# Attention probabilities times values in plain float32, and bias work moved between the engines, in an attention + two-MoE kernel

## The chip, the cores and the metric

The kernel runs on one core of a Trainium2 chip. The metric is device time in microseconds of one execution. A profile gives one execution's span, first to last recorded instruction, and its own time, which is a little longer. The engines are named as in the profile: PE (TensorE matmul), PEld (TensorE weight load), DVE (VectorE), ACT (ScalarE), POOL (GpSimd), SP (the queue that issues most DMAs).

## The reference

Attention with a learned relative-position bias, then two mixture-of-experts layers. The change touches the attention alone:

```python
scores = scale * np.matmul(q, k.transpose(0, 1, 3, 2))
x = (psi_rel / psi_i)[..., None]
bias = np.maximum(x @ w1 + b1, 0.0) @ w2
scores = scores + bias.transpose(2, 0, 1)[None, :, :, :]
attn = np.exp(scores - np.max(scores, axis=-1, keepdims=True))
attn = attn / (np.sum(attn, axis=-1, keepdims=True) + 1e-09)
out = np.matmul(attn, v).astype(np.float32)
```

There are 2 batches, 8 heads, 576 positions and a head width of 64. The result, 1152 rows of 512, goes through `_moe_ref` and `_moe2_ref` (8 experts each, 512 to 1024 to 512).

## The kernel before

**Tiles.** The query rows are cut into 9 tiles of 128: tiles 0 to 7 are one block of 128 positions of one batch each, tile 8 holds the last 64 positions of both batches. Two tiles in a row share one bias block (`it = t // 2`). The loop in `attention` walks over 72 heads (tile, head), and for each one these steps are written out, the scores three heads ahead and the product with V two heads behind:

- `s_mm`: scores, 4 PE matmuls of 288 columns (8 in tile 8), fp32r, Q in two parts against K (L321)
- `s_max`: DVE adds the bias and takes the row maximum (L329)
- `s_exp`: ACT takes the exponential and the row sum (L339)
- `p_turn`: 4 PE transposes of the probabilities, 128x128 float32, into PSUM (L353)
- `p_hi`, `p_lo`: ACT writes the transposed probabilities, times 4096, as float16 (`pth`, L359); DVE writes what float16 left out (`ptl`, L364)
- `av`: for each of 4 chunks of 128 keys, three float16 matmuls of 64 columns: `pth` with VH, `pth` with VL, `ptl` with VH (L382)

The last 64 keys of two neighbouring heads form a "remainder" of 128 rows; it is transposed, split and multiplied once a tile (`av` with h = H, 128 columns). Then `finish` scales by 1/sum (L396), and `x_tile` transposes the tile and makes the router's logits (L683, L692: the latter is a product of two plain float32 operands, 4 matmuls a tile).

**Bias.** The bias of one block is made in 18 pieces of 32 keys (9 in the last block). For each piece DVE makes a mask (L246, L249), PE multiplies it with 16 matmuls into one PSUM tile (L259), and `bias_out` combines it: by default ACT copies it to SBUF (L271) and POOL does a product and a sum (L272, L273); a `direct` piece is read from PSUM by two DVE instructions (L267, L268). Block 0 is made ahead of the loop ("the start"), with pieces 5, 9 and 13 direct; the later blocks are made inside the loop, none direct. The PSUM tile `pm` of the loop has one buffer.

**V and Q.** In the start V is loaded raw (`vraw`, `vrem`), its largest magnitude is found (`v_sums` on ACT, `v_scale`), and `v_split`, `v_rem` write a scaled float16 part on ACT (L302, L310) and the rest on DVE (L303, L311). `q_split` makes Q's fp32r part on ACT (L152) and the low part on POOL (L153). `k_split` does the same for K on ACT and DVE (L166, L167), two pieces in the start and six in the first 11 heads.

**Order.** A scheduler puts the instructions of the loop in a fixed order on each engine; each engine runs its list in order and waits where an operand is not ready. The end of the loop (last heads of tile 8) is in an order written out by hand.

Of the kernel before, what the change touches and what calls it, by code (L numbers as in the profile page):

```python
# [20 lines left out]
BH = B * H
# [6 lines left out]
PSC = 4096.0  # L28
EXPM = 0x7F800000
KCH = 2  # L30
VC = BH * 4 * D // 4
VAT = 11, 13, 15, 17
DIRECT = 5, 9, 13
# [62 lines left out]
def attention(tc, ctx, g, a, out, setup, on_tile, on_slot):  # L96
# [14 lines left out]
    VH = keep.tile([P, BH, 4, D], F16, name="VH")  # L111
    VL = keep.tile([P, BH, 4, D], F16, name="VL")
    VRH = keep.tile([P, BH // 2, 2, D], F16, name="VRH")
    VRL = keep.tile([P, BH // 2, 2, D], F16, name="VRL")
# [35 lines left out]
    def q_split(t):  # L150
        for b, qr, Q in tiles[t].qs:
            nc.scalar.copy(Q[:, 0], qr)  # L152
            nc.gpsimd.tensor_tensor(Q[:, 1], qr, Q[:, 0].bitcast(F32), ALU.subtract)  # L153
# [32 lines left out]
    vraw = prep.tile([P, BH * 4 * D], F32, name="vraw")  # L186
    for x in range(2):
        nc.sync.dma_start(vraw[:, x * 2 * VC:(x + 1) * 2 * VC], a["a_v"][:, x * 2 * VC:(x + 1) * 2 * VC])
    vrem = prep.tile([P, BH // 2, D], F32, name="vrem")
    nc.sync.dma_start(vrem, a["a_vr"].rearrange("p (t d) -> p t d", d=D))  # L190
# [89 lines left out]
    def v_sums(vm, x):  # L280

        junk = prep.tile([P, VC], F16, tag="junk", name="junk", bufs=2)
        src = vraw[:, x * VC:(x + 1) * VC] if x < 4 else vrem.rearrange("p a d -> p (a d)")
        nc.scalar.activation(junk[:, :src.shape[1]], src, AF.Abs, accum_out=vm[:, x:x + 1])

    def v_scale(vm, stage_):
        if stage_ == 0:
            nc.vector.tensor_reduce(vm[:, 5:6], vm[:, 0:5], AX.X, ALU.max)
            v_scale.p = psA.tile([P, 512], F32, tag="acc", name="pv")
            nc.tensor.transpose(v_scale.p[0:1, 0:P], vm[:, 5:6], ident)  # L290
            v_scale.v1 = prep.tile([1, 1], F32, name="v1")
            nc.vector.tensor_reduce(v_scale.v1, v_scale.p[0:1, 0:P], AX.X, ALU.max)
            return
        nc.tensor.matmul(v_scale.p[:, P:P + 1], g.ones[0:1, :], v_scale.v1, start=True, stop=True)
        vmx = prep.tile([P, 1], F32, name="vmx")
        nc.vector.tensor_copy(vmx, v_scale.p[:, P:P + 1])
        return pow2_scales(nc, keep, vmx, "sv")

    def v_split(x):
        cs = slice(x * VC, (x + 1) * VC)  # L300
        vh = VH.rearrange("p a b d -> p (a b d)")[:, cs]
        nc.scalar.mul(vh, vraw[:, cs], sv)  # L302
        nc.vector.scalar_tensor_tensor(VL.rearrange("p a b d -> p (a b d)")[:, cs], vraw[:, cs], sv, vh, ALU.mult, ALU.subtract)  # L303

    def v_rem():
        nc.gpsimd.memset(VRH, 0.0)
        nc.gpsimd.memset(VRL, 0.0)
        for r in range(2):
            rr = slice(r * 64, r * 64 + 64)
            nc.scalar.mul(VRH[rr, :, r], vrem[rr], sv[rr])  # L310
            nc.vector.scalar_tensor_tensor(VRL[rr, :, r], vrem[rr], sv[rr], VRH[rr, :, r], ALU.mult, ALU.subtract)  # L311


# [41 lines left out]
    def p_hi(t, h, ccs=slice(0, 4)):  # L355
        o = tiles[t]
        if h not in o.av:
            o.av[h] = [late.tile([P, 4, P], F16, tag=f"pt{x}", name="pt" + x, bufs=5) for x in "hl"]
        nc.scalar.mul(o.av[h][0][:, ccs], o.pt[h][:, ccs], PSC)  # L359

    def p_lo(t, h, ccs=slice(0, 4)):
        o = tiles[t]
        th, tl = o.av[h]
        nc.vector.scalar_tensor_tensor(tl[:, ccs], o.pt.pop(h)[:, ccs], PSC, th[:, ccs], ALU.mult, ALU.subtract)  # L364

    def av(t, h, ccs=range(4)):
        o = tiles[t]
        if h == 0:
            o.acc = psA.tile([P, 512], F32, tag="acc", name="acc")
        th, tl = o.av[h]  # L370
        for cc in ccs:
            for b, _, _ in o.qs:
                ii = slice(0, P) if t < 8 else slice(b * 64, b * 64 + 64)
                pos = None if t < 8 else (0, b * 64)
                if h < H:
                    cs = slice(h * D, (h + 1) * D)
                    vh, vl = VH[:, b * H + h, cc], VL[:, b * H + h, cc]
                else:
# [73 lines left out]
    for si, u in enumerate(heads[:-4]):  # L452
# [13 lines left out]
        p_lo(*u)  # L466
# [49 lines left out]
    with tc.manual_schedule():  # L516
# [4 lines left out]
        p_hi(t, 4)  # L521
        p_lo(t, 4)
# [3 lines left out]
        p_hi(t, 5)  # L526
        p_lo(t, 5)
# [3 lines left out]
        p_hi(t, 6)  # L531
        p_lo(t, 6)
# [740 lines left out]
```

## Time and profile before

| | |
|---|---|
| median of 3 runs | 659.82 us (657.37 to 660.79) |
| profiled execution, its own time | 658.62 us |
| its span | 656.7 us |
| PE, DVE, ACT, POOL busy in the span | 551.3, 475.0, 400.8, 343.3 us |

The busy time of PE overstates it: matmuls overlap, and one that issues every 0.03 us is shown with a duration of 0.19 us. How long PE is taken by a piece of work is read from the distance between starts. The attention takes the first 256 us of the span.

### The profile page before, as it was taken

What the parts mean: (1) busy time and instruction counts of PE and PEld (TensorE: products, weight loads), DVE (VectorE), ACT (ScalarE), POOL (GpSimd) and SP (SyncE); (2) the same over time, 40 slices, a digit from 0 to 9 for tenths busy, and PEclk for the clock granted to TensorE, in tenths of its full rate; (3) what the DMA queues carried; (4) which work ended last, traced back from release to release, by engine and by line L of the source; (5) the groups of instructions that cost most, each with busy time, mean ns of one, the idle gap of its engine ahead of it and who ended that gap; (6) DMA issues with size and microseconds to landing.
All of it is one profiled execution on the core that took longest, in us unless ns stands there. A gap on an engine that the chain in (4) does not pass through costs nothing. (4 is left out here: it accounts for less than half of the span.)

```text
span 656.7 us, 13255 instructions
## 1 busy us (share of the span) xinstructions
PE 551.3 (84%) x4970; PEld 463.6 (71%) x4970; DVE 475.0 (72%) x702; ACT 400.8 (61%) x668; POOL 343.3 (52%) x290
## 2 busy tenths in 40 slices
PE   2446688887898999679999999989979999999892
PEld 2445577887887887467788788767757887777672
DVE  5789999999998886868951371289679725929660
ACT  4566877887888855358742443378527626648451
POOL 3997899988987262634552141144145513525430
PEclk9977988999999999889999999999999999999797
DMA  7922545101100772298971270168737734847700
GB/s 228 308 74 51 142 133 165 38 30 37 25 18 18 164 267 80 81 324 302 326 284 44 59 252 30 35 211 316 276 102 241 277 126 147 302 150 233 267 8 8
DMA packets 46871, 101.46 MB, mean 154 GB/s; under 512 B 10740, under 2 KB 12660, under 8 KB 46496
## 3 DMA queue, kind: packets, MB, share of 16 engines
q1 hardware_dynamic: 40640, 92.12, 43.2%
q0 software_dynamic: 5232, 7.49, 3.3%
q8 instruction: 64, 1.05, 0.7%
q14 instruction: 55, 0.45, 0.2%
q10 hardware_dynamic: 880, 0.35, 0.2%
HBM read 94.06 MB, written 13.67 MB: 164 GB/s over the span
## 5 line engine op out<-in xcount | busy, mean ns | idle before, releaser
L906 DVE TENSOR_TENSOR wl<-raw,wh 128x1024 fp32r<-128x1024 f32 x106 | 155.1, 1499 | 22.4 <-ACT wh L893 17.4
L959 PE MATMUL py<-wh,hT 128*128 128x512 f32 x400 | 141.4, 404 | 0.3 <-DVE hT L989 0.2
L893 ACT CAST wh<-raw 128x1024 fp32r<-128x1024 f32 x111 | 114.8, 1050 | 12.5 <-ACTq L1161 4.4
L989 DVE TENSOR_TENSOR hT<-pt,hT 128x512 fp32r<-128x512 f32 x50 | 34.5, 691 | 92.7 <-ACT hT L988 92.6
L272 POOL TENSOR_TENSOR btmp<-abst,xp 128x256 f32<-128x256 f32 x78 | 81.0, 1038 | 16.4 <-ACT abst L271 15.2
L959 PEld LDWEIGHTS py<-wh,hT 128*128 128x128 f32 x400 | 75.0, 188 | 16.0 <-DVE hT L989 1.1
L259 PE MATMUL pm<-wmov,mask 128*128 128x64 f16 x1296 | 58.7, 204 | 28.4 <-DVE wmov L234 12.3
L959 PE MATMUL py<-wl,hT 128*128 128x512 f32 x200 | 78.2, 391 | 0.0
L259 PEld LDWEIGHTS <-mask 128*128 128x128 f16 x1296 | 52.9, 106 | 33.5 <-DVE mask L246 22.9
L321 PE MATMUL s<-K,Q 128*128 128x288 f32 x320 | 64.2, 326 | 13.8 <-DVE mx L329 10.3
L273 POOL TENSOR_TENSOR bias<-abst,btmp 128x256 f32<-128x256 f32 x78 | 72.0, 923 | 5.8
L246 DVE TENSOR_TENSOR mask<-toep,T 128x1024 f16<-128x1024 f16 x72 | 69.6, 984 | 0.8 <-PE pm L259 0.5
L339 ACT ACTIVATE P<-sb,mx 128x576 f32<-128x576 f32 x72 | 55.8, 776 | 23.0 <-DVE mx L329 19.3
L271 ACT ACTIVATE abst<-pm,swi 128x512 f32<-128x512 f32 x78 | 53.0, 685 | 21.9 <-PE pm L259 20.6
L959 PE MATMUL ph<-wh,xh 128*128 128x512 f32 x120 | 52.1, 434 | 15.6 <-PEq L1161 10.2
L353 PE MATMUL pt<-ident,P 128*128 128x128 f32 x324 | 53.5, 287 | 9.5 <-DVE ptl L364 6.0
L329 DVE CUSTOM_DVE_ANT_0 sb<-s,bias 128x576 f32<-128x576 f32 x72 | 53.7, 748 | 8.0 <-PE s L321 4.5
L364 DVE SCALAR_TENSOR_TENSOR ptl<-pt,pth 128x512 f16<-128x512 f32 x81 | 54.8, 680 | 5.2 <-ACT pth L359 5.0
L321 PEld LDWEIGHTS s<-K,Q 128*128 128x128 f32 x320 | 47.7, 198 | 15.1 <-issue 9.2
L906 POOL TENSOR_TENSOR wl<-raw,wh 128x1024 fp32r<-128x1024 f32 x22 | 52.7, 2398 | 6.2 <-ACT wh L893 5.5
L359 ACT ACTIVATE pth<-pt 128x512 f16<-128x512 f32 x81 | 47.6, 592 | 8.4 <-PE pt L353 7.1
L988 ACT CAST hT<-pt 128x512 fp32r<-128x512 f32 x50 | 29.4, 587 | 34.3 <-PE pt L983 30.4
(216 smaller groups left out, 1191.0 us busy)
## 6 DMA issues: line engine op xcount, KB each, us to landing
raw<-m_w_dram SPq DMA_DIRECT2D x64, 512.0 KB
raw<-n_w_dram SPq DMA_DIRECT2D x64, 512.0 KB
kraw<-a_k_dram SPq DMA_DIRECT2D x16, 288.0 KB
qraw<-a_q_dram SPq DMA_DIRECT2D x16, 256.0 KB
out_dram<-zero SPq DMA_DIRECT2D x9, 256.0 KB
y_tok<-zero SPq DMA_DIRECT2D x9, 256.0 KB
vraw<-a_v_dram SPq DMA_DIRECT2D x2, 1024.0 KB
x_tok<-x SPq DMA_DIRECT2D x8, 256.0 KB
```

Of the source, the lines that this page charges most:

```text
L246: nc.vector.tensor_tensor(m, w, T[:, i0:i0 + P].unsqueeze(1).to_broadcast([P, 8, P]), ALU.is_gt)
L259: nc.tensor.matmul(pm[:, :, :, gq * 4:gq * 4 + 4], m[:, gq], wmov[:, part], start=part == 0, stop=part == 1)
L272: nc.gpsimd.tensor_tensor(tmp, ab_[:, 0], xp, ALU.mult)
L273: nc.gpsimd.tensor_tensor(biases[it][:, :, cs], ab_[:, 1], tmp, ALU.add)
L321: nc.tensor.matmul(ps[:, half, :288], Q[:, part, h], K[:, b * H + h, half * 288:half * 288 + 288], start=i == 0, stop=i == last)
L329: nc.vector.tensor_tensor_reduce(sb.rearrange("p (t j) -> p t j", t=2), o.ps.pop(h)[:, :, :288], biases[o.it][:, h].rearrange("p (t j) -> ...
L339: nc.scalar.activation(o.Pt[hp][:, x * S:(x + 1) * S], sb, AF.Exp, bias=mx, scale=-1.0, accum_out=o.sums[:, h:h + 1])
L353: nc.tensor.transpose(pt[:, cc], src, ident)
L364: nc.vector.scalar_tensor_tensor(tl[:, ccs], o.pt.pop(h)[:, ccs], PSC, th[:, ccs], ALU.mult, ALU.subtract)
L893: eng.copy(hi, r)
L906: eng.tensor_tensor(lo, self.raw.pop((ge, j)), hi.bitcast(F32), ALU.subtract)
L959: self.nc.tensor.matmul(ps, x[a_][:, xs], w[b_][:, ws], start=first and i == 0, stop=last and i == 2)
```

## The change

The split of V into two float16 parts and the search for its scale are gone: V is loaded as float32 into the tile that the matmuls read (`V_`, and `VR` for the remainder, which is zeroed on POOL and loaded by two DMAs of 64 partitions instead of one of 128). The probabilities are copied from PSUM as float32 by one instruction (`p_out`) on ACT, in the hand-written end for three of the five on DVE; there is no low part. `av` then has one plain float32 matmul for each chunk where there were three in float16. Every second bias piece is `direct` (8 of 18 in the start, every odd one in the loop), and Q's low part is made by DVE for all tiles but the first.

```diff
-DIRECT = 5, 9, 13
+DIRECT = 1, 3, 5, 7, 9, 11, 13, 15
-    VH = keep.tile([P, BH, 4, D], F16, name="VH")
-    VL = keep.tile([P, BH, 4, D], F16, name="VL")
-    VRH = keep.tile([P, BH // 2, 2, D], F16, name="VRH")
-    VRL = keep.tile([P, BH // 2, 2, D], F16, name="VRL")
+    V_ = keep.tile([P, BH, 4, D], F32, name="V")
+    VR = keep.tile([P, BH // 2, 2, D], F32, name="VR")
...
-            nc.gpsimd.tensor_tensor(Q[:, 1], qr, Q[:, 0].bitcast(F32), ALU.subtract)
+            (nc.vector if t else nc.gpsimd).tensor_tensor(Q[:, 1], qr, Q[:, 0].bitcast(F32), ALU.subtract)
...
+    for b in range(B):
+        nc.sync.dma_start(V_[:, b * H:(b + 1) * H].rearrange("p a c d -> p (a c d)"), a["a_v"][:, b * H * 4 * D:(b + 1) * H * 4 * D])
+    nc.gpsimd.memset(VR, 0.0)
+    for r in range(2):
+        rr = slice(r * 64, r * 64 + 64)
+        nc.sync.dma_start(VR[rr, :, r], a["a_vr"][rr].rearrange("p (t d) -> p t d", d=D))
...
+    def p_out(t, h, eng=nc.scalar):
+        o = tiles[t]
+        o.av[h] = late.tile([P, 4, P], F32, tag="pT", name="pT", bufs=5)
+        (eng.copy if eng is nc.scalar else eng.tensor_copy)(o.av[h], o.pt.pop(h))
...
-                for i, (l_, r_) in enumerate(((th, vh), (th, vl), (tl, vh))):
-                    nc.tensor.matmul(o.acc[ii, cs], l_[:, cc, ii], r_, start=h == 0 and cc == 0 and i == 0, stop=i == 2,
-                                     tile_position=pos, skip_group_check=True)
+                nc.tensor.matmul(o.acc[ii, cs], pT[:, cc, ii], v, start=h == 0 and cc == 0, stop=True,
+                                 tile_position=pos, skip_group_check=True)
...
-        nc.vector.tensor_scalar(r, o.sums, 1e-9, PSC, ALU.add, ALU.mult)
+        nc.vector.tensor_scalar(r, o.sums, 1e-9, None, ALU.add)
         nc.vector.reciprocal(r, r)
-        nc.vector.tensor_scalar(r, r, isv, None, ALU.mult)
...
-        if 4 <= x < 9:
-            v_sums(vm, x - 4)
-        if x == 9:
-            v_scale(vm, 0)
-        if x == 10:
-            sv, isv = v_scale(vm, 1)
-        if x in VAT:
-            v_split(VAT.index(x))
-        if x == 16:
-            v_rem()
...
-            bias_out(*w)
+            bias_out(*w, w[1] % 2 == 1)
...
-        p_hi(*u)
+        p_out(*u)
...
-        p_lo(*u)
```

The scheduler gives another order of instructions. Line numbers of the kernel after the change differ from those before. At three places:

On DVE at the end of the start, before the change, up to the first row maximum (`sb,mx`); VL and VRL are the low parts of V:

```order
L267 SCALAR_TENSOR_TENSOR btmp<-pm,swi,xp 128x256
L246 TENSOR_TENSOR mask<-toep,T 128x1024
L268 SCALAR_TENSOR_TENSOR bias<-pm,swi,btmp 128x8x32
L303 SCALAR_TENSOR_TENSOR VL<-vraw,svs,VH 128x1024 x3
L311 SCALAR_TENSOR_TENSOR VRL<-vrem,svs,VRH 64x8x64 x2
L303 SCALAR_TENSOR_TENSOR VL<-vraw,svs,VH 128x1024
L661 COPY enT<-pt 128x32
L329 ISA sb,mx<-s,bias 128x576
```

And the same place after it (L263 and L264 are the direct pieces, L242 the masks, L162 K's low part, L291 the row maximum):

```order
L263 SCALAR_TENSOR_TENSOR btmp<-pm,swi,xp 128x256
L162 TENSOR_TENSOR K<-kraw,K 64x1152
L264 SCALAR_TENSOR_TENSOR bias<-pm,swi,btmp 128x8x32
L242 TENSOR_TENSOR mask<-toep,T 128x1024 x2
L263 SCALAR_TENSOR_TENSOR btmp<-pm,swi,xp 128x256
L242 TENSOR_TENSOR mask<-toep,T 128x1024
L264 SCALAR_TENSOR_TENSOR bias<-pm,swi,btmp 128x8x32
L597 COPY enT<-pt 128x32
L242 TENSOR_TENSOR mask<-toep,T 128x1024
L291 ISA sb,mx<-s,bias 128x576
```

The six instructions on V are gone, and between the masks stand pairs that read a bias piece from PSUM; two of the last masks shown belong to block 1 already. On POOL in the start, `ess` (a small power that DVE needs for `en`) stood behind Q's low part, before the change:

```order
L306 MEMSET VRH 128x1024
L307 MEMSET VRL 128x1024
L153 TENSOR_TENSOR Q<-qraw,Q 128x1024
L653 TENSOR_TENSOR ess<-ess,half 8x1
L272 TENSOR_TENSOR btmp<-abst,xp 128x256
```

and stands ahead of it after the change:

```order
L183 MEMSET VR 128x1024
L589 TENSOR_TENSOR ess<-ess,half 8x1
L148 TENSOR_TENSOR Q<-qraw,Q 128x1024
L268 TENSOR_TENSOR btmp<-abst,xp 128x256
L269 TENSOR_TENSOR bias<-abst,btmp 128x8x32
```

So the small power no longer waits for the long subtraction. On DVE in the loop, at a reciprocal of the row sums in the middle of the attention, before the change (L364 is `p_lo`):

```order
L364 SCALAR_TENSOR_TENSOR ptl<-pt,pth 128x512
L246 TENSOR_TENSOR mask<-toep,T 128x1024
L388 TENSOR_SCALAR rinv<-sums 128x8
L329 ISA sb,mx<-s,bias 128x576
L329 ISA mx 128x1
L364 SCALAR_TENSOR_TENSOR ptl<-pt,pth 128x512
L246 TENSOR_TENSOR mask<-toep,T 128x1024
L389 RECIPROCAL rinv<-rinv 128x8
```

and at such a place after it:

```order
L242 TENSOR_TENSOR mask<-toep,T 128x1024
L148 TENSOR_TENSOR Q<-qraw,Q 128x1024
L263 SCALAR_TENSOR_TENSOR btmp<-pm,swi,xp 128x256
L242 TENSOR_TENSOR mask<-toep,T 128x1024
L264 SCALAR_TENSOR_TENSOR bias<-pm,swi,btmp 128x8x32
L343 TENSOR_SCALAR rinv<-sums 128x8
L344 RECIPROCAL rinv<-rinv 128x8
```

The `ptl` instructions are gone; Q's low part and the direct bias pairs have come, each pair with a mask between its two instructions.

## Rows read from the trace of the kernel before

**Rows 1.** The page: the span.

```profile
span 656.7 us, 13255 instructions
```

**Rows 2.** By stretch: us, busy PE, PEld, DVE, ACT, POOL (x count), PEclk, DMA, GB/s.

```profile
12.00:53.00 41.00, 19.68 (x319) 17.76 (x319) 32.98 (x51) 24.62 (x37) 38.27 (x33) 0.86 0.60 191
53.00:118.80 65.80, 51.06 (x776) 46.03 (x776) 63.81 (x102) 51.30 (x96) 58.09 (x51) 0.91 0.46 122
118.80:205.70 86.90, 74.24 (x1305) 68.72 (x1306) 84.78 (x159) 73.09 (x151) 74.52 (x78) 1.00 0.10 28
205.70:240.30 34.60, 32.79 (x458) 30.49 (x455) 29.03 (x69) 27.00 (x61) 19.24 (x16) 1.00 0.65 189
```

**Rows 3.** Timeline of PE: starts of successive blocks in the loop.

```profile
113.76 0.66 PE L353 MATMUL pt<-ident,P 128*128 128x128 f32 x4 [0.83 <-DVE ptl L364]
114.17 0.78 PE L321 MATMUL s<-K,Q 128*128 128x288 f32 x4
114.79 0.20 PE L382 MATMUL acc<-VH,pth 128*128 128x64 f16 x1
...
115.15 0.22 PE L382 MATMUL acc<-VRH,pth 128*128 128x128 f16 x1
...
115.82 0.63 PE L259 MATMUL pm<-wmov,mask 128*128 128x64 f16 x16
116.29 0.64 PE L353 MATMUL pt<-ident,P 128*128 128x128 f32 x4
```

**Rows 4.** Timeline of PE's weight loads: L692's plain float32 operands, and float16.

```profile
101.67 0.97 PEld L692 LDWEIGHTS s<-enT,xT 128*128 128x128 f32 x8 [1.56 <-DVE mx L329]
...
151.35 0.63 PEld L259 LDWEIGHTS <-mask 128*128 128x128 f16 x16
```

**Rows 5.** All of L692, in the whole span.

```profile
L692 PEld LDWEIGHTS s<-enT,xT x72: 186/192/192, 101.7 to 256.3; 128*128 128x128 f32 x72
```

**Rows 6.** Waits between 118.8 and 205.7 us, in total, times, longest.

```profile
PE acc L382 <- DVE ptl L364: 5.3, 4, 1.5
...
PE pm L259 <- ACT abst L271: 3.3, 4, 1.8
```

**Rows 7.** Timeline of DVE in the start.

```profile
17.05 0.14 DVE L654 TENSOR_SCALAR ess<-ess 8x1 f32<-8x1 f32 x1 [2.79 <-POOL ess L653]
...
18.77 1.89 DVE L246 TENSOR_TENSOR mask<-toep,T 128x1024 f16<-128x1024 f16 x3
20.69 1.77 DVE L167 TENSOR_TENSOR K<-kraw,K 64x1152 fp32r<-64x1152 f32 x1
...
42.40 0.47 DVE L267 SCALAR_TENSOR_TENSOR btmp<-pm,swi,xp 128x256 f32<-128x256 f32 x1
42.79 0.69 DVE L246 TENSOR_TENSOR mask<-toep,T 128x1024 f16<-128x1024 f16 x1
...
53.02 0.76 DVE L329 CUSTOM_DVE_ANT_0 sb<-s,bias 128x576 f32<-128x576 f32 x1 [0.51 <-POOL bias L273]
```

**Rows 8.** POOL's two bias instructions between 12 and 53 us.

```profile
L272 POOL TENSOR_TENSOR btmp<-abst,xp 128x256 f32<-128x256 f32 x15 | 18.0, 1202 | 0.5
L273 POOL TENSOR_TENSOR bias<-abst,btmp 128x256 f32<-128x256 f32 x15 | 16.6, 1108 | 1.2
```

**Rows 9.** DVE between 118.8 and 205.7 us, by line; and a subtraction of Q's shape.

```profile
L246 DVE TENSOR_TENSOR mask<-toep,T 128x1024 f16<-128x1024 f16 x28 | 27.9, 1005 | 0.1
...
L364 DVE SCALAR_TENSOR_TENSOR ptl<-pt,pth 128x512 f16<-128x512 f32 x36 | 24.4, 678 | 0.1
...
L390 DVE TENSOR_SCALAR rinv<-rinv,svi 128x8 f32<-128x8 f32 x4 | 2.6, 655 | 0.0
...
280.22 1.22 DVE L906 TENSOR_TENSOR wl<-raw,wh 128x1024 fp32r<-128x1024 f32 x1
```

**Rows 10.** Timeline of PE in tile 8: first and last row of one head's product.

```profile
241.49 0.23 PE L382 MATMUL acc<-VH,pth 128*64 128x64 f16 x2
...
241.99 0.66 PE L683 MATMUL pt<-ident,x 128*128 128x128 f32 x4
```

More of the change, by code (lines that the diff above doesn't have):

```diff
@@ L27 @@
 NPC = S // 32
-PSC = 4096.0
 EXPM = 0x7F800000
 KCH = 2
-VC = BH * 4 * D // 4
-VAT = 11, 13, 15, 17
-DIRECT = 5, 9, 13
+DIRECT = 1, 3, 5, 7, 9, 11, 13, 15
 XSTEP = 1, 2, 3, 4
@@ L185, in attention @@
     k_load(0)
[L186 to L190, printed above, removed]
+    for b in range(B):
[4 more added lines that the diff above has]
+        nc.sync.dma_start(VR[rr, :, r], a["a_vr"][rr].rearrange("p (t d) -> p t d", d=D))
     k_load(1)
@@ L277, in bias_out @@
             nc.sync.dma_start(biases[4][64:128, :, 0:288], biases[4][0:64, :, 0:288])
[L280 to L311, printed above, removed]
     def s_mm(t, h):
@@ L353, in p_turn, with av @@
             nc.tensor.transpose(pt[:, cc], src, ident)
-    def p_hi(t, h, ccs=slice(0, 4)):
+    def p_out(t, h, eng=nc.scalar):
         o = tiles[t]
[L357 to L366, printed above, removed]
+        o.av[h] = late.tile([P, 4, P], F32, tag="pT", name="pT", bufs=5)
+        (eng.copy if eng is nc.scalar else eng.tensor_copy)(o.av[h], o.pt.pop(h))
+    def av(t, h):
         o = tiles[t]
@@ L369, in av @@
             o.acc = psA.tile([P, 512], F32, tag="acc", name="acc")
-        th, tl = o.av[h]
-        for cc in ccs:
+        pT = o.av.pop(h)
+        for cc in range(4):
             for b, _, _ in o.qs:
@@ L376, in av @@
                     cs = slice(h * D, (h + 1) * D)
-                    vh, vl = VH[:, b * H + h, cc], VL[:, b * H + h, cc]
+                    v = V_[:, b * H + h, cc]
                 else:
                     cs = slice(cc * P, (cc + 1) * P)
-                    vh, vl = (V_[:, b * 4 + cc].rearrange("p t d -> p (t d)") for V_ in (VRH, VRL))
-                for i, (l_, r_) in enumerate(((th, vh), (th, vl), (tl, vh))):
-                    nc.tensor.matmul(o.acc[ii, cs], l_[:, cc, ii], r_, start=h == 0 and cc == 0 and i == 0, stop=i == 2,
-                                     tile_position=pos, skip_group_check=True)
+                    v = VR[:, b * 4 + cc].rearrange("p t d -> p (t d)")
+                nc.tensor.matmul(o.acc[ii, cs], pT[:, cc, ii], v, start=h == 0 and cc == 0, stop=True,
+                                 tile_position=pos, skip_group_check=True)
     def recip(t):
@@ L403, in attention @@
     rot = (psM, "pm"), (psT, "pt"), (psT, "pt"), (psS, "s"), (psS, "s")
-    vm = prep.tile([P, 6], F32, name="vm")
     for x in range(NPC + 2):
@@ L475, in attention @@
         if rem:
-            p_hi(t - 1, H)
+            p_out(t - 1, H)
         for w in two:
-            bias_out(*w)
+            bias_out(*w, w[1] % 2 == 1)
         if lead:
@@ L481, in attention @@
         if rem:
-            p_lo(t - 1, H)
             recip(t - 1)
@@ L520, in attention @@
         s_max(t, 7)
-        p_hi(t, 4)
-        p_lo(t, 4)
+        p_out(t, 4)
         av(t, 2)
@@ L525, in attention @@
         p_turn(t, 5)
-        p_hi(t, 5)
-        p_lo(t, 5)
+        p_out(t, 5, nc.vector)
         s_exp(t, 7)
@@ L530, in attention @@
         p_turn(t, 6)
-        p_hi(t, 6)
-        p_lo(t, 6)
+        p_out(t, 6, nc.vector)
         recip(t)
@@ L535, in attention @@
         p_turn(t, 7)
-        p_hi(t, 7)
-        p_lo(t, 7)
+        p_out(t, 7)
         p_turn(t, H, psS)
-        p_hi(t, H)
+        p_out(t, H, nc.vector)
         av(t, 5)
-        p_lo(t, H)
         av(t, 6)
```

## The prediction

> **What bounds the kernel now.** I read the busy times by stretch first; the stretches end where the `finish` of tiles 1, 5 and 7 starts. The attention falls into stretches with different limits. Between 118.8 and 205.7 us, tiles 2 to 5, DVE is busy 84.8 of 86.9 us while PE has gaps [rows 2]: a tile takes 21.7 us and DVE sets it. The same holds from 53 to 118.8 (63.8 of 65.8), where K's low parts come on top. From 205.7 to 240.3, tiles 6 and 7, no bias is left but three pieces and a tile takes 17.3 us; PE comes nearest to its full share. In the start (12 to 53) POOL is busy 38.3 of 41 us, and the first row maximum waits for a bias piece of POOL [rows 2, 7].
>
> How long PE is really taken must be read from starts in the timeline. Successive blocks in the loop [rows 3]: 4 transposes 0.41 us (113.76 to 114.17), scores 0.62, product with V 0.36, remainder's product 0.67, 16 matmuls of a bias piece 0.47. A head is 0.41 + 0.62 + 0.36 + 18/16 x 0.47 = 1.92 us; a tile is 8 of them, plus the remainder's transposes and product (1.08), and `x_tile`'s 4 transposes (0.41) and 8 passes of L692 (0.89, below): 15.4 + 2.4 = 17.8 us. So PE has 3.9 us of waits in each tile of 21.7 us. The list of waits says for whom: 5.3 us in the four tiles before the product alone for `ptl`, p_lo's result on DVE, and 3.3 for the PSUM tile of a bias piece [rows 6].
>
> **The product with V (PE).** Three float16 matmuls of 64 columns become one plain float32 matmul. The trace of before has one such operation, L692. It has 36 of them in the program and 72 weight loads in the trace [rows 5]: a plain float32 matmul is two passes, each with its own weight load. Eight passes take 0.97 us with the last load's 0.19 in it, so one starts every 0.78 / 7 = 0.111 us, although only 8 columns stream [rows 4]. Float16 loads of the same size start every (0.63 - 0.10) / 15 = 0.035 us or faster [rows 4] (0.36 / 12 = 0.030 in the product with V [rows 3]). A transposing pass, which loads 128x128 float32 and streams 128 float32 columns, takes 0.41 / 4 = 0.10 us: 64 columns fit under a load. So a head's product becomes 4 x 2 x 0.111 = 0.89 us instead of 0.36, +0.53; the remainder (8 passes too) 0.89 instead of 0.67, +0.22; a tile +4.5 us, to 22.3 us of PE. The lower end is that 0.10 a pass (+3.7), the upper a score pass, 0.62 / 4 = 0.155 for 288 columns (+7.6); 0.111 is the only row of the same operation, so I take it.
>
> [...]
>
> **DVE in the loop.** Gone: 9 `ptl` a tile at 0.61 us (0.678 less the overlap with the next, 0.07) [rows 9], -5.5. Added: half of 9 bias pieces, two instructions each at 0.39 (42.40 to 42.79 [rows 7]), +3.5; Q's low part, 1.22 us for a subtraction of the same shape [rows 9], +1.2 (up to 1.5 beside a busy POOL). The masks take 1.00 us here [rows 9] and 0.69 or 0.63 where POOL is quiet [rows 7]; POOL's work is more than halved (the bias pieces by half, Q's low part gone), and I count 0.2 less for each, -1.8. DVE's 21.2 us a tile [rows 2] become about 18.6. ACT, at 73.1 of 86.9 us [rows 2], loses half of the bias copies; `p_out` is p_hi's instruction with another output type.
>
> So in tiles 2 to 5 the bound passes from DVE (21.2) to PE (22.3). The waits for `ptl` go: `p_out` on ACT is all that the product needs. But two engines at 84% and more of the pace, in fixed orders, don't mesh without loss; I take 0.7 us of waits. 23.0 against 21.7, four tiles: **+5.2 us**. Ends: no waits and the lower pass, 21.5 (-0.8), to the upper pass, 25.4 (+15).
>
> **Tiles 6 and 7.** PE's work: two times 8 x 1.39 + 2.4, three bias pieces (1.4) and 12 more score matmuls for the first three heads of tile 8 (3 x 0.62): 30.3 us of 34.6. With +9.0 it is 39.3, and with half of the 4.3 us of waits left, 41.5: **+7.0** (ends +4.5 without waits, +9 with all).
>
> **Tile 8.** Two products of 64 output rows stand side by side in the array: 24 float16 matmuls take 0.50 us (241.49 to 241.99 [rows 10]). After, there are 16 passes, with weights of 64 columns. Between half of 0.111 for each (0.89 us, if loads follow one another) and half of that (0.45, if neighbours overlap as now). Nearer to rows 10, where neighbours overlap: 8 heads at +0.15 and the remainder, **+1.5** (0 to +4). The end loses a `ptl` from its chain, which I set against the waits there.
>
> **The start.** Gone are the sums, scales and parts of V, which stood ahead of the first row maximum on DVE and ACT without being needed by it. What it needs is block 0's bias. POOL has 15 pieces at 2.31 us (1.20 + 1.11 [rows 8]); after, 10. `ess` now stands ahead of Q's low part on POOL, so DVE's wait of 2.79 us goes [rows 7] and its masks, which went on at 18.77, do so at 16.0. From there DVE has 14 masks of block 0 (0.85 each, between 0.63 and 1.0), 7 direct pieces (0.8 each) and two K parts (1.77 each [rows 7]): the last two masks are done at 36 and 37. Pieces 16 and 17 both go by PE, ACT and POOL: I count 1.5 us for the first two, then 2 x 2.31 on POOL, so the bias is complete at 42, against 53.02 [rows 7]: **-11.0**. Ends: with POOL at its quiet pace and masks at 0.7, -13; with masks at 1.05, -8. V's bytes are the same; the two remainder DMAs write runs of 256 bytes and stand ahead of K's second load, with some 14 us until that is used.
>
> **53 to 118.8.** DVE stays the bound (PE: some 40 us of work and +9.5 in 65.8). Gone: 20 `ptl` (two tiles, three heads, one remainder), -12.1. Added: 13 direct pieces +10.3 and four low parts of Q +5.2. Masks: 25 (block 1's 18 and the first of block 2's) at 0.2 less, -5.0; two are already made while the last bias pieces finish, -1.5. The third small instruction of the reciprocal, twice 0.66 less the overlap [rows 9], -1.2. Together **-4.3** (0 to -8).
>
> **Sum.** -11.0 - 4.3 + 5.2 + 7.0 + 1.5 = -1.6. Behind 256 us nothing changes; the experts' weights are requested from the same heads on. The profiled execution took 658.62 us (span 656.7 and 1.9 around it [rows 1]), so 657.0; that is 1.2 under the median of the three runs, 659.82, as the profiled one was itself. 0.5% is 3.3 us, about what a measurement of this kernel can tell from no change.
>
> **The rivals.** (1) *The PSUM tile of a bias piece is held by DVE.* It has one buffer. ACT frees it in one instruction; a direct piece is free after two on DVE with a mask between them (0.39 + 0.61 to 1.0 + 0.39), and later if DVE's queue is behind. PE already waits 3.3 us for it [rows 6]. If every direct piece of tiles 2 to 5 (18) costs PE 1 us, it ends at 672; if every second, 665. It decides from 5 us on. For it: PE is now the bound, so each wait counts. Against: a piece is mostly a whole head old when the next one is made. Slower; chance 0.22. (2) *PE's waits vanish.* Most of those listed are for `ptl` [rows 6], which is gone. Tiles 2 to 5 at 22.3 (+2.4), tiles 6 and 7 +4.5, tile 8 0, the start -13: 658.6 - 10.4 = 648. Against: two nearly full engines. 0.18. [...] 0.05. (4) *The start isn't shorter by more than 6*: the order of DMAs, or POOL fed late by masks that wait for PSUM tiles: 662. 0.05.
>
> **How the numbers follow.** My forecast, 657.0, has 0.50, with its own range 651 to 663 (by the ends of the start and of tiles 2 to 7, each less likely the further out). Inside it 0.38 lies under 655.3, 0.07 over 661.9. Faster: 0.19 + 0.18 + 0.05 = 0.42. Slower: 0.22 + 0.03 = 0.25, and 0.01 of the last rival. Same: 0.32. For 8 in 10 the range takes in rival 2 and rival 1 where every second piece waits: 645 to 668.
>
> **What the profile of the changed kernel would show.** L337's weight loads: 640 and more of them, one every 0.11 us, a head's product at 0.89 us. The first row maximum (L291) at 42 us, with a wait for POOL or none. From there to the second `finish` 61 us with DVE busy nearly throughout; then tiles of 23 us with DVE below 85%, and waits of PE mostly for `pm` and scores, none for p_lo. Tiles 6 and 7 at 20.8. A product much under 0.8 us a head, tiles 2 to 5 over 24, or a first row maximum after 46 would make the prediction wrong.

## The result, and the profile after

The changed kernel takes 654.19 us (median of 9 runs, 652.79 to 655.66) against 659.82 of the kernel before (9 runs beside it, 657.37 to 661.0): ratio 0.9916, 95% interval 0.9896 to 0.9935. The profiled execution took 655.32 us, 3.3 less than that of before. By the terms of the sum:

| stretch | before | after | difference | predicted |
|---|---|---|---|---|
| to the first row maximum | 53.0 | 45.0 | -8.0 | -11.0 |
| from there to the second `finish` | 65.8 | 63.7 | -2.1 | -4.3 |
| tiles 2 to 5 | 86.9 | 89.9 | +3.0 | +5.2 |
| tiles 6 and 7 | 34.6 | 40.5 | +5.9 | +7.0 |
| tile 8 | 12.8 | 13.0 | +0.2 | +1.5 |
| behind the attention | 403.6 | 401.4 | -2.2 | 0 |

So the attention ends only 1.0 us earlier: 10 us are gained ahead of tile 2, and 9 are given back in the tiles behind. By stretch (us, busy PE, PEld, DVE, ACT, POOL with counts, PEclk, which is the granted share of TensorE's clock, DMA share, GB/s), cut where [rows 2] is cut:

```profile
12.00:45.00 33.00, 19.95 (x319) 17.44 (x319) 28.94 (x49) 11.84 (x17) 23.74 (x23) 0.74 0.77 230
45.00:108.70 63.70, 54.74 (x633) 51.45 (x634) 53.34 (x99) 43.07 (x82) 19.07 (x21) 0.92 0.47 131
108.70:198.60 89.90, 89.36 (x1187) 87.26 (x1186) 73.53 (x159) 64.18 (x135) 32.38 (x38) 1.00 0.10 27
198.60:239.10 40.50, 40.50 (x427) 40.11 (x426) 21.78 (x58) 27.72 (x61) 15.81 (x15) 1.00 0.51 149
```

In tiles 2 to 5 the bound has passed from DVE (73.5 of 89.9 us busy now) to PE, which now fills tiles 6 and 7 too. In the second stretch neither is full. The starts on PE in the loop, which answer to [rows 3]:

```profile
122.53 0.55 PE L337 MATMUL acc<-V,pT 128*128 128x64 f32 x4
122.92 0.63 PE L255 MATMUL pm<-wmov,mask 128*128 128x64 f16 x16
123.38 0.64 PE L337 MATMUL acc<-V,pT 128*128 128x64 f32 x4
123.86 0.61 PE L315 MATMUL pt<-ident,P 128*128 128x128 f32 x4
124.22 0.77 PE L283 MATMUL s<-K,Q 128*128 128x288 f32 x4
124.83 0.55 PE L337 MATMUL acc<-V,pT 128*128 128x64 f32 x4
```

A head's product stands in two halves of 4 passes, 0.39 and 0.48 us: 0.87, 0.109 a pass. Its weight loads in tiles 2 to 5, by form (count, busy us, mean ns), are 256 for 128 matmuls, 192 ns each; a float16 load takes half as long, 99 ns:

```profile
L337 PEld LDWEIGHTS acc<-V,pT 128*128 128x128 f32 x256 | 32.2, 192 | 0.0
L255 PEld LDWEIGHTS <-mask 128*128 128x128 f16 x577 | 21.2, 99 | 1.3 <-issue 0.3
```

The recorded matmuls are 256 too, two for each of the program's 128.

The start, DVE and then POOL, against [rows 7, 8]:

```profile
12.62 1.91 DVE L242 TENSOR_TENSOR mask<-toep,T 128x1024 f16<-128x1024 f16 x3
14.99 0.14 DVE L590 TENSOR_SCALAR ess<-ess 8x1 f32<-8x1 f32 x1 [0.47 <-POOL ess L589]
15.06 2.94 DVE L599 CAST wg<-wgr 128x32 fp32r<-128x32 f32 x1
...
19.41 1.08 DVE L242 TENSOR_TENSOR mask<-toep,T 128x1024 f16<-128x1024 f16 x1
...
38.67 1.85 DVE L242 TENSOR_TENSOR mask<-toep,T 128x1024 f16<-128x1024 f16 x2
...
45.05 0.76 DVE L291 CUSTOM_DVE_ANT_0 sb<-s,bias 128x576 f32<-128x576 f32 x1 [2.21 <-POOL bias L269]
```

```profile
12.62 2.34 POOL L589 TENSOR_TENSOR ess<-ess,half 8x1 f32<-8x1 f32 x1 [10.27 <-ACT esq L588]
14.95 2.33 POOL L148 TENSOR_TENSOR Q<-qraw,Q 128x1024 fp32r<-128x1024 f32 x1
...
41.55 0.73 POOL L268 TENSOR_TENSOR btmp<-abst,xp 128x256 f32<-128x256 f32 x1 [1.59 <-ACT abst L267]
42.36 1.05 POOL L269 TENSOR_TENSOR bias<-abst,btmp 128x256 f32<-128x256 f32 x1
43.49 0.72 POOL L268 TENSOR_TENSOR btmp<-abst,xp 128x256 f32<-128x256 f32 x1
44.29 0.72 POOL L269 TENSOR_TENSOR bias<-abst,btmp 128x256 f32<-128x256 f32 x1
```

The long wait for `ess` is gone, but the masks still go on only at 19.4: DVE's small copy `wg` takes 2.94 us while POOL's subtraction runs. The last two pieces follow one another on POOL, and the row maximum waits 2.2 us for them. Waits in the second stretch (in total, times, longest):

```profile
PE pm L255 <- DVE bias L264: 3.1, 3, 2.1
...
DVE K L162 <- ACT K L161: 2.7, 1, 2.7
PE s L283 <- DVE K L162: 2.6, 3, 1.3
```

The first is the mechanism of rival 1. In tiles 2 to 5 the list has one kind of wait for PE, and it isn't for `pm` but for DVE's row maximum:

```profile
PE s L283 <- DVE mx L291: 0.5, 2, 0.3
```

### The profile page after: what moved, and what is told of

Its sections match the earlier page's. It is cut to its first block, busy times and chain, and to the rows that moved or that the text cites. A ratio compares the mean times of both kernels' runs of the same rounds, so it can differ in the third digit from the quotient of the medians.

```text
span 653.5 us, 12410 instructions
## 1 busy us (share of the span) xinstructions
PE 578.3 (88%) x4607; PEld 498.4 (76%) x4607; DVE 437.3 (67%) x682; ACT 369.5 (57%) x613; POOL 246.7 (38%) x208
## 5 line engine op out<-in xcount | busy, mean ns | idle before, releaser
L842 DVE TENSOR_TENSOR wl<-raw,wh 128x1024 fp32r<-128x1024 f32 x106 | 152.5, 1474 | 20.9 <-ACT wh L829 18.4
L255 PE MATMUL pm<-wmov,mask 128*128 128x64 f16 x1296 | 58.1, 204 | 26.3 <-DVE wmov L230 12.6
L268 POOL TENSOR_TENSOR btmp<-abst,xp 128x256 f32<-128x256 f32 x42 | 35.6, 849 | 117.7 <-ACT abst L267 109.5
L337 PE MATMUL acc<-V,pT 128*128 128x64 f32 (+1 forms) x640 | 72.6, 263 | 0.6 <-DVE x L350 0.6
L291 DVE CUSTOM_DVE_ANT_0 sb<-s,bias 128x576 f32<-128x576 f32 x72 | 53.5, 752 | 29.0 <-PE s L283 12.0
L337 PEld LDWEIGHTS acc<-V,pT 128*128 128x128 f32 (+1 forms) x640 | 68.4, 182 | 1.9 <-issue 1.0
L242 DVE TENSOR_TENSOR mask<-toep,T 128x1024 f16<-128x1024 f16 x72 | 56.0, 783 | 6.7 <-PE pm L255 6.3
L320 ACT COPY pT<-pt 128x512 f32<-128x512 f32 x78 | 44.5, 582 | 26.8 <-PE pt L315 26.5
L315 PE MATMUL pt<-ident,P 128*128 128x128 f32 x324 | 52.0, 283 | 1.5 <-ACT P L301 1.2
L267 ACT ACTIVATE abst<-pm,swi 128x512 f32<-128x512 f32 x42 | 28.6, 684 | 38.7 <-PE pm L255 36.4
```

The costliest lines, as they stand in the source:

```text
L242: nc.vector.tensor_tensor(m, w, T[:, i0:i0 + P].unsqueeze(1).to_broadcast([P, 8, P]), ALU.is_gt)
L255: nc.tensor.matmul(pm[:, :, :, gq * 4:gq * 4 + 4], m[:, gq], wmov[:, part], start=part == 0, stop=part == 1)
L268: nc.gpsimd.tensor_tensor(tmp, ab_[:, 0], xp, ALU.mult)
L291: nc.vector.tensor_tensor_reduce(sb.rearrange("p (t j) -> p t j", t=2), o.ps.pop(h)[:, :, :288], biases[o.it][:, h].rearrange("p (t j) -> ...
L315: nc.tensor.transpose(pt[:, cc], src, ident)
L320: (eng.copy if eng is nc.scalar else eng.tensor_copy)(o.av[h], o.pt.pop(h))
```

## The experiments

All against the kernel before on the same chip. The stretches are from the profiled executions, cut at the same marks; "end" is the last `finish`, "behind" the rest of the span.

| run | median us | ratio (95% interval) | first maximum | to 2nd finish | tiles 2-5 | 6-7 | end | behind |
|---|---|---|---|---|---|---|---|---|
| changed kernel | 654.19 | 0.9916 (0.9896-0.9935) | 45.0 | 63.7 | 89.9 | 40.5 | 252.1 | 401.4 |
| e1 loop by ACT | 648.83 | 0.9847 (0.9822-0.9873) | 44.6 | 62.1 | 87.6 | 40.1 | 247.3 | 398.2 |
| e2 three direct | 656.78 | 0.9965 (0.9937-0.9993) | 49.0 | 62.7 | 89.9 | 40.6 | 255.2 | 399.7 |
| e3 before, eight direct | 655.05 | 0.9945 (0.9925-0.9964) | 50.7 | 66.0 | 88.3 | 34.8 | 252.6 | 400.6 |
| e4 product fp32r | 653.30 | 0.9904 (0.9867-0.9941) | 55.4 | 61.1 | 85.6 | 37.4 | 252.1 | 402.5 |
| e5 before, moves | 661.80 | 1.0034 (1.0015-1.0053) | 52.9 | 66.0 | 92.9 | 37.9 | 263.0 | 399.1 |
| e7 last direct | 654.09 | 0.9917 (0.9890-0.9943) | 45.1 | 65.9 | 89.9 | 40.6 | 254.4 | 399.6 |
| e8 first Q on DVE | 653.03 | 0.9898 (0.9870-0.9925) | 42.9 | 63.8 | 89.9 | 40.6 | 250.1 | 401.0 |
| e9 fp32r, loop by ACT | 633.31 | 0.9602 (0.9562-0.9643) | 44.4 | 57.7 | 80.5 | 32.9 | 228.5 | 401.7 |
| e0 changed, again | 653.79 | 0.9922 (0.9895-0.9949) | 44.8 | 63.7 | 89.8 | 40.6 | 251.9 | 398.6 |
| e12 before, again | 660.92 | 1.0008 (0.9986-1.0029) | 52.9 | 65.8 | 86.9 | 34.4 | 252.8 | 406.6 |
| e10 e1 + e8 | 644.82 | 0.9777 (0.9746-0.9807) | 42.7 | 61.0 | 87.6 | 39.8 | 244.1 | 400.3 |
| e11 e9 + e8 | 629.94 | 0.9552 (0.9524-0.9580) | 42.6 | 58.1 | 80.5 | 32.9 | 227.1 | 401.1 |

**e1: no direct pieces in the loop.**

```diff
-            bias_out(*w, w[1] % 2 == 1)
+            bias_out(*w)
```

> The changed kernel, but no bias piece of the loop is direct: ACT copies each and POOL combines it, as before the change; the start keeps its eight direct pieces. Theory (in tiles 2 to 7 PE alone sets the pace, and the direct pieces only moved work between engines that have time): DVE loses 3.5 us a tile and gets back some of it in slower masks, ACT gains 2.7 on 16.0; tiles 2 to 5 stay at 22.5 us each within 0.3, tiles 6 and 7 at 20.2. Between the first row maximum and the second finish, where PE waits 3.1 us for the PSUM tile held by direct pieces and neither engine is full, 1 to 3 us may be gained or lost. Total 651 to 656. Rival (the direct pieces hold the one PSUM tile and cost PE time everywhere): tiles 2 to 5 fall to 22.0 or under and the total to 650 or under.

The rival is nearer: tiles 2 to 5 take 21.9 us each instead of 22.5, and the total is 5 us under the changed kernel. By stretch:

```profile
44.55:106.60 62.05, 54.41 (x667) 51.42 (x668) 50.60 (x80) 48.12 (x93) 47.27 (x46) 0.92 0.42 114
106.60:194.20 87.60, 87.60 (x1192) 86.64 (x1188) 67.51 (x122) 75.64 (x155) 64.67 (x75) 1.00 0.15 40
```

PE is busy in all of 87.60 us; ACT and POOL have time for the work that DVE gave back. Of the 4.8 us by which the attention ends earlier, 2.3 come from tiles 2 to 5 and 1.6 from the stretch before them. I had taken PE's share of 89.36 in 89.90 as proof that no wait was left; the 2.3 us that e1 gains there show neither in that share nor in the list, which has 0.5. The granted clock is the same in both runs (0.92, then 1.00), so it is no part of this. Through which wait the direct pieces cost tiles 2 to 5, e1 doesn't show.

**e2 and e3: which edit shortened the start.** e2 is the changed kernel with the old list, e3 the kernel before with the new one.

```diff
-DIRECT = 1, 3, 5, 7, 9, 11, 13, 15
+DIRECT = 5, 9, 13
```

> The changed kernel, but the start has three direct pieces (5, 9, 13) as before the change. Theory (the start is set by POOL, and the move of bias pieces to DVE is what shortened it): POOL has 15 pieces at about 2.3 us again, 34 us from 17 on, so the first row maximum comes at 51 to 52 us against 45.0, everything behind it as in the changed kernel, total 660 to 661. Rival (the start became shorter because V's sums and parts left DVE and ACT): the first row maximum stays under 47, total under 656.5.

> The kernel before, float16 parts of V and all, with one edit: eight direct pieces in the start (1, 3, ... 15). Theory (both parts are needed: POOL is relieved by the direct pieces, but DVE, busy 33 of 41 us, then has 4 us more on top of V's parts): first row maximum at 48.5 to 50 us against 53.0, total 655.5 to 657. Rival (the direct pieces alone do it, V's work fits beside): first row maximum at 45 to 46, total 652. Other rival (they only move the load, DVE then is what ends last): first row maximum at 52 or later, total 659.

Neither end holds: without the direct pieces the first maximum is at 49.0, with them alone at 50.7. Of the 8.0 us, V's sums and parts leaving gives 4.0 alone, the direct pieces 2.3 alone, and 1.7 come only with both, each kernel in the order that the scheduler gives it. In e2 POOL is the busiest engine of the start (34.96 of 37.00 us), in e3 DVE (33.21 of 38.73).

```profile
12.00:49.00 37.00, 22.03 (x332) 19.51 (x332) 27.81 (x39) 14.97 (x22) 34.96 (x32) 0.64 0.63 190
```

```profile
12.00:50.73 38.73, 20.90 (x303) 17.73 (x302) 33.21 (x58) 22.31 (x33) 26.91 (x23) 0.63 0.69 216
```

The granted clock differs between the starts as well: 0.86 before and 0.74 in the changed kernel, 0.64 and 0.63 here. In the kernel before it is no term of the sum: e12, the same kernel, had 1.00 and its first row maximum at 52.9. For e2 and e3 no run shows it.

```profile
12.00:52.89 40.89, 21.94 (x319) 19.61 (x318) 32.85 (x49) 24.77 (x38) 38.01 (x33) 1.00 0.61 192
```

**e4 and e9: half the passes, with and without direct pieces.** Both have the product's operands in fp32r for tiles 0 to 7. e9 has e1's edit as well, and V comes on SP's queue and is copied to fp32r by ACT.

```diff
-    V_ = keep.tile([P, BH, 4, D], F32, name="V")
+    V_ = keep.tile([P, BH, 4, D], F32R, name="V")
...
-        o.av[h] = late.tile([P, 4, P], F32, tag="pT", name="pT", bufs=5)
+        o.av[h] = late.tile([P, 4, P], F32R, tag="pT", name="pT", bufs=5)
...
+                if t == 8:
+                    l, v = l.bitcast(F32), v.bitcast(F32)
```

> The changed kernel with the product's operands as fp32r in tiles 0 to 7 (tile 8 stays plain float32): low-order bits of probabilities and V are left out, and V is loaded by POOL's queue instead of SP's, since that load rounds. Theory (PE sets tiles 2 to 7, and what it takes there is two float32 weight loads per matmul): if fp32r needs one pass of the same 0.107 us, a head's product falls from 0.86 to 0.43 us, a tile's PE time by 3.9 to 18.6; DVE's 18.4 is then just as long, tiles 2 to 5 take 19.5 to 20.5, tiles 6 and 7 16.5 to 17.5, total 636 to 643. Rival (not the product but the fixed orders and DVE set the pace): the product becomes shorter and tiles 2 to 5 stay over 22, total 651 to 655. If fp32r takes as many passes as float32 at 64 columns, nothing moves and the run tells nothing on this.

> The kernel with the product in fp32r (low-order bits of probabilities and V left out in tiles 0 to 7) and without direct pieces in the loop; V comes in on SP's queue and ACT rounds it, four copies of 1024 columns and two small ones in the start. Theory (with the product in one pass PE has time to spare, and what the run with direct pieces lost again, 17.8 us of PE waits in tiles 2 to 5, 10.7 of them listed for a bias piece that DVE still held, was the price of the direct pieces): those waits fall under 8 us, tiles 2 to 5 take 19.6 to 20.6 us each against 21.4 with direct pieces, total 634 to 642. Rival (the waits come from DVE's queue as such and remain): tiles 2 to 5 stay at 21.2 or more, total over 645.

In e4 the loads fall to half, at the same 0.19 us each:

```profile
L340 PEld LDWEIGHTS acc<-V,pT 128*128 128x128 f32 x128 | 17.9, 191 | 0.0
```

and PE waits, in tiles 2 to 5, for the bias piece that DVE holds:

```profile
PEld L255 <- DVE bias L264: 6.3, 10, 1.2
...
PE pm L255 <- DVE bias L264: 4.4, 10, 1.1
```

The two rows are the same ten waits, seen by the weight loads and by the matmuls; the expectation of e9 added them, which was wrong. Tiles 2 to 5 come down to 21.4 us only, and DVE's hold on `pm` now shows. In e9 a tile takes 20.1 us and the whole 633.3; in place of the waits for DVE it has some for ACT. From the first row maximum to the last `finish` it takes 184.1 us, e4 196.7.

```profile
PE pm L257 <- ACT abst L269: 5.2, 7, 1.5
```

Tiles 2 to 5 and tiles 6 and 7, first e4, then e9:

```profile
116.40:202.10 85.70, 79.40 (x1040) 75.06 (x1040) 76.44 (x159) 63.60 (x135) 32.36 (x38) 0.96 0.10 28
202.10:239.50 37.40, 35.00 (x357) 34.17 (x357) 21.76 (x59) 27.28 (x61) 13.67 (x13) 0.95 0.53 155
```

```profile
102.10:182.60 80.50, 74.05 (x1048) 71.50 (x1045) 67.46 (x125) 74.64 (x155) 69.49 (x75) 1.00 0.16 43
182.60:215.50 32.90, 32.01 (x324) 31.44 (x321) 17.52 (x50) 27.77 (x63) 14.40 (x15) 1.00 0.63 177
```

The two don't show the price of direct pieces, as I had meant them to. In tiles 2 to 5 PE stands still for 6.30 us in e4 and for 6.45 in e9; what became shorter is its busy time. A part of that can be the clock's: e4 was granted 0.96 and 0.95, e9 1.00, which by my estimate is worth up to 3.4 us (0.04 x 85.7) of the 5.2 between the first lines, and up to 1.9 (0.05 x 37.4) of the 4.5 between the second. Why e4's clock fell no run shows. The product's price is read from e1 and e9, both without direct pieces in the loop and at 1.00: tiles 2 to 5 fall from 87.6 to 80.5 us, tiles 6 and 7 from 40.1 to 32.9. So PE's passes are the bound of the changed kernel's tiles.

e4's start is worse (55.4): V's loads stand on another queue there, and DVE waits 7.3 us for a small load (`cap`); the start was not what it was made for.

**e5: the moves alone, with the float16 product.** The kernel before with `bias_out(*w, w[1] % 2 == 1)` in the loop and Q's low part on DVE from tile 1 on.

> The kernel before, float16 parts and all, with the other half of the change: every odd bias piece of the loop direct, Q's low part on DVE; the start keeps its three direct pieces. Theory (DVE sets the loop of the kernel before, so work moved to it costs its own length there): per tile +3.5 us for the direct pieces, +1.2 for Q's low part, -1.8 from quicker masks, tiles 2 to 5 at 24 us instead of 21.7 (+9 to +10 in all), the stretch up to the second finish +8, the start unchanged at 53; total 672 to 680. Rival (the moves alone are a gain, POOL's relief being worth more than DVE's load): total 658 or less, tiles 2 to 5 under 21.7.

The direction in tiles 2 to 7 is the theory's (+6.0 and +3.3), its size is not, and the stretch up to the second `finish` grew by 0.2 only. The masks became cheaper than I counted: 0.73 us, where [rows 9] has 1.00.

```profile
L246 DVE TENSOR_TENSOR mask<-toep,T 128x1024 f16<-128x1024 f16 x28 | 20.3, 732 | 0.0
```

```profile
118.90:211.80 92.90, 81.44 (x1328) 73.05 (x1328) 91.66 (x197) 65.27 (x134) 32.42 (x37) 0.98 0.12 35
```

DVE, busy 91.7 of 92.9 us, is the bound there. In tiles 6 and 7 the granted clock was 0.92 against 1.00 before [rows 2], so a part of the 3.3 can be the clock's (an estimate: up to 3.0, 0.08 x 37.9). The attention ends 9.9 us later, the median is only 2.0 up; the part behind is 4.5 shorter, see e12.

**e7 and e8: the two faults of the start.**

```diff
-DIRECT = 1, 3, 5, 7, 9, 11, 13, 15
+DIRECT = 1, 3, 5, 7, 9, 11, 13, 15, 17
```

```diff
-            (nc.vector if t else nc.gpsimd).tensor_tensor(Q[:, 1], qr, Q[:, 0].bitcast(F32), ALU.subtract)
+            nc.vector.tensor_tensor(Q[:, 1], qr, Q[:, 0].bitcast(F32), ALU.subtract)
```

> The changed kernel, but the last bias piece of the start, 17, is direct too. Theory (the first row maximum waits 2.2 us for POOL because pieces 16 and 17 follow one another there): piece 16 is done on POOL at 43.4, piece 17 on DVE before that; first row maximum at 43.4 against 45.0, total 1.6 us under the changed kernel. Rival (DVE, busy from 19 to 42 us almost throughout, is what the start waits for): first row maximum at 45 or later, total the same.

> The changed kernel, but Q's low part is made by DVE for the first tile too. Theory (DVE's copy of wg took 2.94 us only because POOL's subtraction ran beside it): with POOL idle there the copy takes 0.2 to 0.6 us, the subtraction 1.2 on DVE, so the masks go on at 17.5 to 18.0 us instead of 19.4 and the first row maximum comes at 43.5 against 45.0. Rival (the copy is slow by itself): it still takes over 2.5 us, the masks go on at 20.5, the first row maximum at 46.

e7 moved the wait: the direct piece waits for POOL's piece 16, and two masks of the next block stand between it and the row maximum, which comes at 45.1 again. The second stretch is 2.2 us longer than in the changed kernel, with a granted clock of 0.84 there against 0.92; no run separates the two.

```profile
42.73 0.48 DVE L263 SCALAR_TENSOR_TENSOR btmp<-pm,swi,xp 128x256 f32<-128x256 f32 x1 [0.93 <-POOL bias L269]
43.13 0.69 DVE L242 TENSOR_TENSOR mask<-toep,T 128x1024 f16<-128x1024 f16 x1
43.73 0.47 DVE L264 SCALAR_TENSOR_TENSOR bias<-pm,swi,btmp 128x256 f32<-128x256 f32 x1
44.12 1.05 DVE L242 TENSOR_TENSOR mask<-toep,T 128x1024 f16<-128x1024 f16 x1
45.09 0.74 DVE L291 CUSTOM_DVE_ANT_0 sb<-s,bias 128x576 f32<-128x576 f32 x1
```

e8 held: the subtraction takes 1.23 us on DVE, the masks go on at 17.5, and the row maximum comes at 42.9. The copy now stands at 38.2, where POOL has no instruction, and takes 0.15.

```profile
13.01 1.23 DVE L148 TENSOR_TENSOR Q<-qraw,Q 128x1024 fp32r<-128x1024 f32 x1 [0.62 <-ACT Q L147]
...
17.48 0.68 DVE L242 TENSOR_TENSOR mask<-toep,T 128x1024 f16<-128x1024 f16 x1
...
38.20 0.15 DVE L599 CAST wg<-wgr 128x32 fp32r<-128x32 f32 x1
...
42.86 0.76 DVE L291 CUSTOM_DVE_ANT_0 sb<-s,bias 128x576 f32<-128x576 f32 x1 [2.33 <-POOL bias L269]
```

**e0 and e12: both kernels again, unchanged.**

> The changed kernel once more, word for word, for a second profile. Theory (of the 3.3 us between the first two profiles, 2.3 lie behind the attention in code that the change doesn't touch, in one gap of PE at a branch that a given execution has or hasn't): the attention ends within 0.5 us of 252.1 and the part behind it differs from 401.4 by 1 to 3 us. Rival (that part is shorter in the changed kernel for good): it lasts 401.4 within 0.5 us.

> The kernel before once more, word for word, for a second profile. Theory (the gap at the branch belongs to an execution): the last finish comes at 253.1 within 0.5 us, the part behind it lasts 398 to 402 us without a wait of 3 us for PE's sequencer. Rival (the gap belongs to the kernel before): 403.6 us within 0.5, with the same wait of 3 us at the same place.

The attention repeats within 0.3 us. Behind it, the two profiles of each kernel lie 3 us apart (403.6 and 406.6; 401.4 and 398.6), so e0 came as its theory had it, and e12 with neither of its times. A part goes with the kernel: both profiles of before have a wait of 3.0 and 3.4 us of PE for its own sequencer at a branch of the last experts, in neither of the changed kernel is one there; both kernels have another, of 3.2 to 3.6, further ahead. The waits in the last experts, first before, then before again:

```profile
PE ph L959 <- PEq L1161: 3.0, 1, 3.0
```

```profile
PE ph L959 <- PEq L1161: 3.4, 1, 3.4
```

and the same stretch of the changed kernel:

```profile
PE ph L895 <- PEq L1097: 0.7, 1, 0.7
```

e5, with V's parts in float16, has none over 0.8 us, so it doesn't go with the product. The code there is the same in all; what differs is what stands ahead of it, and not by the number of matmuls and weight loads: it is 4970 of each in the kernel before, and e5's edit adds and removes none. Why PE waits at that branch no run here shows.

**e10 and e11: the edits that helped, together.**

> The changed kernel, still with a plain float32 product, without direct pieces in the loop and with Q's low part on DVE for the first tile too: the two edits that helped, together. Theory (the one acts in the start, the other in the loop): first row maximum at 42.9, tiles 2 to 5 at 21.9 us, total 2 us under the run without direct pieces in the loop, 646 to 648. Rival (what the start gains is lost in the stretch up to the second finish, where waits for bias pieces and K set the pace): first row maximum at 42.9, second finish still at 106.6, total 649.

> The kernel with the product in fp32r (low-order bits of probabilities and V left out in tiles 0 to 7) and no direct pieces in the loop, plus Q's low part on DVE for the first tile too. Theory: first row maximum 1.6 to 2.2 us earlier than 44.4, tiles 2 to 5 at 20.1 us as without that edit, total 631 to 632.5. Rival (lost again before the second finish): second finish at 102 as before, total 633.

Both beat the changed kernel: e10, with the plain float32 product, by 9.4 us (ratio 0.9777 to before), e11, with fp32r, by 24 (0.9552). In e10 the start's 1.8 us stay, and 1.1 more come before the second `finish`; in e11 the first maximum gains 1.9 and the second `finish` 1.5.

## Why the prediction came out as it did

The total was forecast at 657.0 and is 654.2, in the range and on the side that had the largest chance. Each term's sign was right and each size too large; the last term, forecast at nothing, was not nothing. That the sum came this near is in part luck: the two stretches ahead of tile 2 gave 5.2 us less than forecast, the tiles behind cost 4.6 less, and 2.2 came from code that the change doesn't touch.

**Product with V.** Forecast 0.89 us a head, measured 0.87. Two passes with a float32 weight load each, from L692's rows, was right, and e9 against e1 shows it from the other side: half as many loads, and a tile comes down from 21.9 to 20.1 us. Of the 0.42 for faster, 0.05 stood for a cheaper float32 product, at a price that no run shows; what the runs show is 256 loads for 128 matmuls and 0.87 us a head.

**Tiles 2 to 7.** The bound passed to PE as forecast. A head takes 0.36 + 0.61 + 0.87 + 0.52 = 2.36 us of PE (transposes, scores, product, bias), a tile 8 times that plus 2.5 for the remainder and `x_tile`, 21.4, where I had 22.3. The waits are then 1.1 us a tile, where I took 0.7. The step that was mis-sized is PE's work: the transposes were taken at 0.41 us a head and took 0.36, the product at 0.89 and took 0.87. DVE fell to 73.53 / 4 = 18.4 us a tile, forecast 18.6; its masks came at 0.78 us, near the 0.80 counted, but for a reason that the rows don't bear out: the masks in [rows 7] ran beside POOL instructions, not beside a quiet POOL, those of 0.63 us beside one of 2.71 and the one of 0.69 beside one of 1.16 (see the last section).

**Rival 1** I had as another case with the time of 665 or more. A part of it is in the case that came: up to the second `finish` PE waits 3.1 us for pieces that DVE holds, and e1, without direct pieces in the loop, gains 4 of its 4.8 us ahead of tile 6. In tiles 2 to 5 the hold itself isn't shown, since no wait for `pm` is listed there; e4 shows it, 4.4 us of waits in four tiles, when PE has less to do. Rival 2 was nearer than the forecast in the tiles: 22.5 us in tiles 2 to 5 against its 22.3 and my 23.0, +0.2 in tile 8 against its 0. Its total of 648 failed on the start, which it had at -13. Rival 4 is out, the start being 8 us shorter.

**The start.** The step that failed is that with `ess` ahead of Q's low part DVE's wait of 2.79 us goes and the masks go on at 16.0. The wait went, but `ess` itself took 2.34 us on POOL, and the `wg` copy, to which I had given no price, took 2.94 us beside POOL's subtraction; the masks went on at 19.4. That is the whole of the 3 us: from there to the last mask I had 21 us, and it took 40.5 - 19.4 = 21.1. e8 gives 2.2 of it back by taking the subtraction off POOL. The copy ended at 18.0, 0.7 us behind the subtraction; in e8, where no POOL instruction runs beside it, it took 0.15. How the subtraction makes it longer no run shows.

**To the second finish.** Forecast -4.3 with DVE busy nearly throughout; measured -2.1 with DVE busy 53.3 of 63.7 us. The step that failed is that DVE stays the bound. Its work fell by 10.5 us, since the masks cost 0.76 instead of the 0.82 counted, K's low parts 1.42 instead of 1.82, and only 10 direct pieces fell into the stretch, not 13. The first tile of it became 4.6 us shorter (36.4 against 41.0), the second 2.6 longer (27.3 against 24.7), with one wait of PE of 2.1 us for a piece that DVE held. In e1 they take 40.1 and 22.0: without direct pieces in the loop the first is longer and the second shorter. The granted clock is 0.91 and 0.94 in the two tiles, 0.87 and 1.00 in e1's, so what each tile gains or loses isn't the pieces' alone.

**Tile 8.** Forecast +0.15 us a head; a product takes 0.62 us where [rows 10] has 0.50, so +0.12; the stretch grew by 0.2 only.

**Behind the attention.** "Nothing changes" is the last step that failed. Of the 5.6 us between the medians, 1.0 is in the attention by the profiles. The rest lies in code that the change doesn't touch; the wait at one branch makes up about 2.5 of it. What sets it stays open.

## What to carry to other kernels

The plain float32 matmul of 64 columns took two weight loads here and 0.109 us a pass, about what L692 takes for 8 columns (0.111): count passes by the nearest plain float32 row. In fp32r, where the precision allows it, half of the loads were left (e4: 128 for 128 matmuls), and a tile came from 21.9 us (e1) to 20.1 (e9). An engine with time to spare is no free place for work if PE waits for that engine, as for the single PSUM buffer that DVE held here (3.1 us up to the second `finish`): DVE was busy 73.5 of 89.9 us in tiles 2 to 5, and the work given back to ACT and POOL was worth 5 us. Before two runs are set against each other, their granted clocks have to be: of the 13 us between e4 and e9 in the attention, up to 8 can be the clock's (granted 0.92 over it in e4, 0.96 in e9; an estimate, 0.04 x 196.7). A gain that lies in removing one wait has to name what runs beside the instruction that comes next: here `wg`, at 2.94 us, took the place of a wait of 2.79.

## What the runs showed that I had not expected

A small instruction took as long as a large neighbour on the other engine. DVE's `wg` copy of 128x32 took 2.94 us beside POOL's subtraction of 2.33 and 0.15 alone (e8). POOL's `ess`, 8x1, took 2.34 us beside DVE's three masks of 1.91 in the changed kernel and 0.64 in e8, where they stand later:

```profile
12.20 0.64 POOL L589 TENSOR_TENSOR ess<-ess,half 8x1 f32<-8x1 f32 x1 [9.85 <-ACT esq L588]
```

Which of two neighbours took longer differed. In e8 three masks took 2.96 us beside POOL instructions of 1.22 and 1.06. In the kernel before, the three that start at 18.77 took 0.63 each, and POOL's product of a bias piece 2.71 us beside them, where it had 0.72 just ahead of them, at 17.00:

```profile
18.53 2.71 POOL L272 TENSOR_TENSOR btmp<-abst,xp 128x256 f32<-128x256 f32 x1
```

And an edit of one stage moved the time of another that it doesn't touch by some 3 us, in part through waits at branches whose place differs from kernel to kernel and repeats in two profiles of the same one (3.0 and 3.4 us in the last experts of the kernel before, 0.7 at most in the changed one).
